# Sign rows by memset, channel angles ahead of the fold, and shared channel copies in a Fourier mixing and low-rank mixer kernel

## The chip, the cores and the metric

The kernel runs on one core of a Trainium2 chip. The metric is the device time of one execution in microseconds (us). Before the change it was 492.16 us, the median of three runs (491.61 to 494.13).

## The reference

```python
def _attn_ref(x):                       # x: 8 x 3136 x 256, float32
    X = np.fft.fft(x, axis=1)
    X = np.fft.fft(X, axis=2)
    return X.real

def _moe_ref(x, U, V, w_ch1, w_ch2):    # x: the output of the above
    xt = x.transpose(0, 2, 1)
    h = xt @ U @ V                      # U: 3136 x 32, V: 32 x 3136
    u = x + h.transpose(0, 2, 1)
    ch = np.maximum(u @ w_ch1, 0.0) @ w_ch2   # 256 -> 1024 -> 256
    return u + ch
```

For each of eight batches, the real part of a two-dimensional Fourier transform is taken; then a rank-32 mixing along the sequence is added, and then a two-layer network over the channels.

## The kernel before

**The Fourier part as products.** The sequence transform is a matrix product with cosine and sine tables that the kernel makes itself at its start: `tabs` (two tiles, sine `tabs` and cosine `tabc`, of 99 partitions by 8 by 2 by 425). Columns up to `NQ` = 393 hold the trigonometric values, the last 32 hold the tables' product with U, so one product gives the transform and U's part of the low-rank path together. VectorE computes the angles (`phase`: a multiply-add, then a mask on the integer bits, two instructions), ScalarE takes the sines (`sine`) and, with Abs before it, the cosines (`cosine`). Symmetries save sines: `mirror_even` fills half of a row from the other half, and `cosine_odd`, `cosine_low`, `cosine_high` copy sine values reversed into the cosine table. `turned_copy` gives a copy with sign + to GpSimd and one with sign - to ScalarE. `halve` scales one row of a table on VectorE. `fold_u` and `transform_u` contract U with the tables on TensorE.

**Folding x.** The rows of x come in twice, forward (`xf`, by an indirect gather issued by GpSimd) and reversed (`xr`); a 99th partition holds the edge row (`load_0f`, `load_0r`). VectorE folds along the channels (`along_d`, L303 and L305, into `EOF_` and `EOR_`), GpSimd converts two columns that stand alone (`alone`, L309), VectorE folds along the sequence (`mirror`, L312, into `EOS`), and `half` (L316) gives `G`, the stationary operand of the sequence product.

**One batch.** `transform(b)` yields eight `seq` groups (L352; each pair of groups is evicted by ScalarE into `ev` at L356 and combined by VectorE at L359, L366 and L368 or L370 into `tab`, `A` and `B`), then eight `chan` steps (L467 and L469, with the channel tables `MC` and `MSN`; each result is copied out of PSUM at L471 into `S` or `T`), then `lowrank` (L479, with `MSN` and `MC`; the result goes into `TA` at L485); in batch 0 `lowrank` stands ahead of the `chan` steps. PSUM tiles of the tag `dft` rotate through three buffers. Row 0 of `MSN` is replaced by alternating signs (L687, L688) after its sines. `TA[s]` is the stationary operand of the low-rank product with `VA[s]` (V and two more rows); its rows 32 and 33 are written by `ta_rows`: a clear, a copy of two rows of alternating signs from `alt` (L641), then a row of zeros and two single elements.

**The stream.** `front(c)` forms a chunk of 512 rows: the low-rank product `ph` (L511) plus `S` or `T` on VectorE (L519) gives `u`, which a DMA also transposes. `first_product` (L531, relu on ScalarE at L533) and `second_product` (L547, added up on VectorE at L553 to L556) are the network. Steps of the next batches (its fold, its transform, the loads of the batch after it) are spread between the products of the chunks by `spread`.

**Order.** Up to the first chunk the order of each engine's queue is the program's own (`manual_schedule`); from the second chunk on a scheduler may move instructions, with the folds and loads pinned. Every engine works through its queue in order. The loads of batch 1 and of the weights and V are issued by GpSimd, between its copies and memsets:

```python
    load_r(1, 0)
    load_f(1, 0)
    along_d(1, xr, EOR_, 1)
    load_r(1, 1)
    av = alt.rearrange("p (l two) -> p l two", two=2)
    nc.gpsimd.memset(av[:, :, 0:1], 1.0)
    nc.gpsimd.memset(av[:, :, 1:2], -1.0)
    ta_rows(0)
```

In the built program the copy at L641 carries waits for the landing of a gather of x (for `ta0` that of `load_f(1, 0)`, for `ta1` that of `load_f(1, 1)`), beside the wait for GpSimd's own clear.

Of the kernel before, what the change touches and what calls it, by code (L numbers as in the profile page):

```python
# [20 lines left out]
NQ = 393  # L21
# [6 lines left out]
def kernel(  # L28
# [227 lines left out]
    def halve(t):  # L256
        nc.vector.tensor_single_scalar(tabs[t][:, NI - 1, :, :NQ], tabs[t][:, NI - 1, :, :NQ],
                                       hv[:KP], op=AL.mult)

    def cells(t, i, col, step, n, skew):  # L260

        v = tabs[t][:, i, :, :]
        return bass.AP(v.tensor, v.offset + col, [v.ap[0], [QW + skew, 2], [step, n]])

    def turned_copy(dst, src, sgn):

        if sgn > 0:
            nc.gpsimd.tensor_copy(dst, src)  # L268
        else:
            nc.scalar.activation(dst, src, AF.Copy, scale=-1.0)  # L270
# [6 lines left out]

    def cosine_odd(i):

        turned_copy(cells(1, i, 1, 1, NQ - 1, 0), cells(0, i, NQ - 2, -1, NQ - 1, 1),  # L280
                    1 if i % 4 == 0 else -1)

    def cosine_low(i):

# [22 lines left out]
    def alone(a, src, dst):  # L307

        pin(nc.gpsimd.tensor_copy(dst[:, a, :, 128:257:128], src[:, a, :, 0:129:128]))  # L309
# [67 lines left out]
    GC = [cpool.tile([KP, NI, NB], BF16, name=f"gc{par}", tag=f"gc{par}") for par in range(2)]  # L377
    rows = cpool.tile([NB, S], BF16, name="rows")
    tabc128 = cpool.tile([NB, NB, R], BF16, name="tabc128")
    alt = cpool.tile([P, 256], BF16, name="alt")  # L380
    flip = cpool.tile([P, 2, P], BF16, name="flip")
    unit = cpool.tile([P, NB], FP32, name="unit")

# [78 lines left out]
    def chan(b, ch, h):  # L462
        d = ST[b]
        lo = ch * 392 + (1 if ch else 0)
        hi = (ch + 1) * 392 + 1
        pt = psum.tile([P, NQ], FP32, tag="dft", name="pst", bufs=3)
        nc.tensor.matmul(pt[:, :hi - lo], MC[:, h * P:(h + 1) * P], d["A"][:, lo:hi],  # L467
                         start=True, stop=False)
        nc.tensor.matmul(pt[:, :hi - lo], MSN[:, h * P:(h + 1) * P], d["B"][:, lo:hi],  # L469
                         start=False, stop=True)  # L470
        nc.scalar.copy(d["ST"[h]][:, lo:hi], pt[:, :hi - lo])  # L471

    def lowrank(b):
        d = ST[b]
# [129 lines left out]
            mirror_even(0, 3)  # L604
    cosine_low(1)
    mirror_even(0, 1)
    for i in (0, 4):
        cosine_odd(i)
    halve(0)
    nc.vector.tensor_copy(GU[:, 0], pf[0][:])  # L610
    pf.append(fold_u(1))
    nc.vector.tensor_single_scalar(sel.rearrange("p a c -> p (a c)"),
# [2 lines left out]
    us[0]()  # L615
    cosine(tabs[1][:, 7, :, NH - 1:NQ], phe[:, 0], 15)
    nc.scalar.copy(cells(1, 7, 0, 1, NH - 1, 1), cells(1, 7, NQ - 1, -1, NH - 1, 0))
    nc.scalar.copy(GU[:, 1], pf[1][:])
    us[1]()
    us[2]()  # L620
# [2 lines left out]
    cosine_low(5)  # L623
    cosine_high(1)
    us[3]()
    alone(0, xr, EOR_)
    alone(0, xf, EOF_)
    nc.gpsimd.iota(pint[:], pattern=[[0, 1]], base=D, channel_multiplier=-1)  # L628
# [3 lines left out]
    w1t = gen.tile([P, H], FP32, name="w1t", tag="w1t", bufs=1)  # L632
    gather(w1t[:], moe_w_ch1, D, pint[:], H, 0)
    alone(1, xf, EOF_)
    nc.gpsimd.memset(VA[0][:].bitcast(I32), 0)
    nc.gpsimd.dma_start(out=VA[0][:R, :], in_=moe_V)
    nc.gpsimd.dma_start(out=W2[:], in_=moe_w_ch2.rearrange("(j p) d -> p j d", p=P))

    def ta_rows(s):
        nc.gpsimd.memset(TA[s][:].bitcast(I32), 0)  # L640
        nc.gpsimd.tensor_copy(TA[s][R:R + 2, :], alt[R:R + 2, :])  # L641
        nc.gpsimd.memset(TA[s][R:R + 1, :], 0.0)
        nc.gpsimd.memset(TA[s][R:R + 1, 0:1], 1.0)
        nc.gpsimd.memset(TA[s][R:R + 1, P:P + 1], -1.0)

    for part in range(2):
        along_d(0, xr, EOR_, part)
    along_d(0, xf, EOF_, 0)
    mirror(0, slice(0, 128), AL.subtract)
    along_d(0, xf, EOF_, 1)  # L650
    mirror(0, slice(128, 258), AL.add)
    halve(1)
    for step in uc:
        step()
    along_d(1, xr, EOR_, 0)
    along_d(1, xf, EOF_, 0)
    mirror(1, slice(0, 128), AL.subtract)
# [6 lines left out]
    load_f(1, 0)  # L664
    along_d(1, xr, EOR_, 1)
    load_r(1, 1)
    av = alt.rearrange("p (l two) -> p l two", two=2)
    nc.gpsimd.memset(av[:, :, 0:1], 1.0)
    nc.gpsimd.memset(av[:, :, 1:2], -1.0)
    ta_rows(0)  # L670
    along_d(1, xf, EOF_, 1)
    mirror(1, slice(128, 256), AL.add)
    for par in range(2):
        half(0, par, slice(128, 256))
    nc.vector.memset(lrow[:, 1, 0:1], 128.0)
    nc.vector.tensor_single_scalar(pcol[:], pcol[:], 1.0 / D, op=AL.mult)
    pd = gen.tile([P, 2 * P], I32, name="pd", bufs=1)
    phase(pd[:], lrow.rearrange("p a l -> p (a l)"), pcol[:], 17)
    sine(MSN[:, 0:128], pd[:, 0:128], 17, -1)
    sine(MSN[:, 128:256], pd[:, 128:256], 17, 1)  # L680
    cosine(MC[:], pd[:], 17)
    msr = MSN[0:1].rearrange("p (l two) -> p l two", two=2)
    MDT = [MSN, MC]
    load_f(1, 1)
    load_0f(x, xf, 1, D, nc.gpsimd)
    load_0r(x, xr, 1, D, nc.gpsimd)
    nc.gpsimd.memset(msr[:, :, 0:1], 1.0)  # L687
    nc.gpsimd.memset(msr[:, :, 1:2], -1.0)  # L688
    nc.gpsimd.tensor_copy(W1[:, 1, :], w1t[:])
    ta_rows(1)  # L690
    column_zeros()
    for par in range(2):
        nc.gpsimd.memset(G[1][par][:, :, 258:GW].bitcast(I32), 0)
# [80 lines left out]
```

## Time and profile before

| | |
|---|---|
| median of three runs | 492.16 us (491.61 to 494.13) |
| profiled execution | 492.97 us |
| its span, first to last instruction | 491.2 us |
| mean granted TensorE clock | 0.979 |
| TensorE (PE) busy | 462.7 us, 94% |
| VectorE (DVE) busy | 314.4 us, 64% |
| ScalarE (ACT) busy | 282.3 us, 57% |
| GpSimd (POOL) busy | 70.2 us, 14% |

The lines that follow come from one profiled execution. In a timeline a row is: start in us from the span's start, length in us, engine, source line, operation, output<-inputs, shape, count, and in brackets the idle time before it with what ended it. In the list of waits a row is: who waited <- for whom: us in total, times, the longest. In the windows a row is: the stretch, its length, the busy time of PE, PEld (weight loads), DVE, ACT and POOL with their instruction counts, the mean granted TensorE clock, the mean busy share of the 16 DMA engines and GB/s. A matmul row's end is modelled, so lengths of rows overlap where matmuls follow each other; starts are safer.

### The profile page before, as it was taken

To read this page: it belongs to the slowest core of one execution; us is meant where nothing else is said; L and a number is where in the kernel's file an instruction comes from. 1 tells how busy PE (TensorE), PEld (TensorE's weight loads), DVE (VectorE), ACT (ScalarE), POOL (GpSimd) and SP (SyncE) were. 2 spreads that over 40 slices of the span, in tenths; PEclk is the share of its full clock that TensorE was granted. 3 is DMA by queue.
4 is the path that set the end of the run, shared out by engine and by line. 5 is a ranking of instruction groups with operands and counts; after the bars stand their busy time and mean duration, and the time that the engine had idled before them with its cause. 6 is when DMAs were issued, how large, how long until landed. Compare 5 with 4: busy or idle time off the path is not lost.

```text
span 491.2 us, 7944 instructions
## 1 busy us (share of the span) xinstructions
PE 462.7 (94%) x2979; PEld 295.3 (60%) x3033; DVE 314.4 (64%) x709; ACT 282.3 (57%) x534; POOL 70.2 (14%) x122
## 2 busy tenths in 40 slices
PE   4683999999999999999999999999999999999997
PEld 2431465665566666666666666666666666666665
DVE  8971797676677756786477657776569643344343
ACT  7621753665566655665566555655566556665562
POOL 4943431020001200121011200130000000000000
PEclk9877899999999999999999999999999999999999
DMA  7596398997347953767356833785233423343433
GB/s 197 119 193 176 62 213 150 216 179 164 66 117 190 218 87 107 196 184 143 84 146 184 220 85 87 197 224 104 84 89 78 118 64 87 107 87 108 129 87 128
DMA packets 103606, 67.24 MB, mean 137 GB/s; under 512 B 73546, under 2 KB 100068, under 8 KB 100416
## 3 DMA queue, kind: packets, MB, share of 16 engines
q1 hardware_dynamic: 97722, 40.69, 36.8%
q0 software_dynamic: 5824, 26.03, 19.9%
q8 instruction: 23, 0.38, 0.3%
q14 instruction: 15, 0.12, 0.1%
q10 hardware_dynamic: 22, 0.02, 0.0%
HBM read 29.33 MB, written 25.69 MB: 112 GB/s over the span
## 4 chain that ended last, share of the span: by engine, by line
PE 86%; DVE 5%; POOL 3%; DMA 3%; issue 2%; ACT 1%; DVEq 0%; POOLq 0%
PE p L547 34%; PE p L531 31%; PE pt L352 9%; PE ph L511 4%; DMA xf<-in_x_dram,xidx 3%; PE pst L467 3%; PE pst L469 2%; PE ptt L479 1%; PE ptc L438 1%; DVE u L519 1%; ACT tabs L177 1%; DVE pho L172 1%; POOL tabc L268 1%; DVE pho L170 0%; DVE eof L305 0%
## 5 line engine op out<-in xcount | busy, mean ns | idle before, releaser
L533 ACT ACTIVATE h<-p 128x512 bf16<-128x512 f32 x392 | 224.6, 599 | 153.7 <-PE p L531 145.1
L531 PE MATMUL p<-u,w 128*128 128x512 bf16 x732 | 208.5, 379 | 1.2 <-DVE u L519 0.3
L547 PE MATMUL p<-w,h 128*128 128x256 bf16 x1568 | 203.1, 273 | 1.5
L547 PEld LDWEIGHTS <-h 128*128 128x128 bf16 x1568 | 153.1, 98 | 59.4 <-DVE o L556 0.3
L531 PEld LDWEIGHTS <-w 128*128 128x128 bf16 x784 | 75.5, 98 | 53.6 <-issue 2.7
L553 DVE TENSOR_TENSOR o<-p,ut 128x4 f32<-128x4 f32 (+1 forms) x100 | 16.4, 164 | 93.1 <-PE p L547 87.6
L352 PEld LDWEIGHTS <-g 98*128 98x128 bf16 (+1 forms) x288 | 28.7, 100 | 30.8 <-issue 4.7
L359 DVE TENSOR_TENSOR tab<-pt,ev 128x32 bf16<-128x32 f32 x32 | 6.1, 191 | 59.1 <-PE pt L352 57.0
L55 POOL DMA_INDIRECT xf<-in_x_dram,xidx x16 | 17.8, 1110 | 170.6 <-DVE eof L305 160.5
L519 DVE TENSOR_TENSOR u<-ph,S 128x512 bf16<-128x512 f32 (+15 forms) x64 | 34.9, 554 | 11.2 <-ACT T L471 11.2
L555 DVE TENSOR_TENSOR o<-p,ut 128x254 f32<-128x254 f32 (+1 forms) x100 | 40.5, 405 | 0.0
L556 DVE TENSOR_TENSOR o<-p,ut 128x254 f32<-128x254 f32 (+1 forms) x100 | 40.4, 404 | 0.0
L352 PE MATMUL pt<-tabc,g 98*128 98x425 bf16 (+1 forms) x160 | 36.2, 355 | 0.2
L519 DVE TENSOR_TENSOR u<-ph,T 128x512 bf16<-128x512 f32 (+15 forms) x64 | 34.8, 554 | 0.0
L352 PE MATMUL pt<-tabs,g 98*128 98x425 bf16 (+1 forms) x128 | 30.0, 358 | 2.5 <-DVE g L316 1.7
L511 PE MATMUL ph<-va,ta 128*128 128x512 bf16 (+13 forms) x126 | 29.3, 332 | 0.1
L356 ACT COPY ev<-pt 128x425 f32<-128x425 f32 x32 | 16.4, 515 | 16.6 <-PE pt L352 15.4
L467 PE MATMUL pst<-A,mc 128*128 128x392 bf16 (+1 forms) x64 | 22.3, 348 | 0.3
L312 DVE TENSOR_TENSOR eos<-eof,eor 99x1024 bf16<-99x1024 bf16 (+2 forms) x33 | 22.3, 688 | 0.3 <-POOL pint L628 0.2
L469 PE MATMUL pst<-B,msn 128*128 128x392 bf16 (+1 forms) x64 | 22.2, 347 | 0.0
L316 DVE TENSOR_TENSOR g<-eos 99x2064 bf16<-99x2064 bf16 (+2 forms) x20 | 19.9, 1011 | 0.1
L303 DVE TENSOR_TENSOR eof<-xf 99x1016 bf16<-99x1016 f32 x16 | 19.9, 1244 | 0.0
(136 smaller groups left out, 300.8 us busy)
## 6 DMA issues: line engine op xcount, KB each, us to landing
out_dram<-o SPq DMA_DIRECT2D x48, 512.0 KB
xr<-in_x_dram POOLq DMA_DIRECT2D x14, 784.0 KB, 6.6
xr<-in_x_dram SPq DMA_DIRECT2D x2, 784.0 KB
ut<-u SPq DMA_TRANSPOSE x49
w<-in_moe_w_ch_dram POOLq DMA_DIRECT2D x1, 512.0 KB, 8.0
out_dram<-o SPq DMA_DIRECT2D x4, 128.0 KB
va<-in_moe_V_dram POOLq DMA_DIRECT2D x2, 196.0 KB, 3.7
xf<-in_x_dram,xidx POOLq DMA_INDIRECT x16, 7.2
```

The costliest lines, as they stand in the source:

```text
L303: pin(nc.vector.tensor_tensor(dst[:, a, :, 1:128], lo, hi, op=AL.subtract))
L312: pin(nc.vector.tensor_tensor(EOS[:, a, :, cols], EOF_[:, a, :, cols], EOR_[:, a, ::-1][:, :, cols], op=op))
L352: nc.tensor.matmul(pt[:], g[:kp(i), i, col:col + P], tabs[t][:kp(i), i, par, :], start=(n == 0), stop=(n == len(mm) - 1))
L467: nc.tensor.matmul(pt[:, :hi - lo], MC[:, h * P:(h + 1) * P], d["A"][:, lo:hi], start=True, stop=False)
L469: nc.tensor.matmul(pt[:, :hi - lo], MSN[:, h * P:(h + 1) * P], d["B"][:, lo:hi], start=False, stop=True)
L511: nc.tensor.matmul(ph[:, col:col + hi - lo], TA[b % 2][:, s * P:(s + 1) * P], VA[b % 2][:, lo:hi], start=True, stop=True)
L519: nc.vector.tensor_tensor(u[:, s, col:col + hi - lo], ph[:, col:col + hi - lo], src, op=AL.add)
L531: nc.tensor.matmul(p1[:], W1[:, s, j * P:(j + 1) * P], k["u"][:, s, :], start=(s == 0), stop=(s == 1))
L533: LAST[0] = nc.scalar.activation(k["h"][:, j, :], p1[:], AF.Relu)
L547: nc.tensor.matmul(p2[:, t % w, :], h[:, j, rs], W2[:, j, :], start=(j == 0), stop=(j == JT - 1))
L555: nc.vector.tensor_tensor(o[:, ts, 1:P], p2[:, :w, 1:P], ut[:, ts, 1:P], op=AL.add)
L556: nc.vector.tensor_tensor(o[:, ts, P + 1:D], p2[:, :w, P + 1:D], ut[:, tT, P - 1:0:-1], op=AL.add)
```

## The change

- `alt`, both `TA` tiles' constant rows and `VA[0]`'s clear are written right after the other constants, in GpSimd's queue ahead of its first table copies; the two rows of alternating signs in `TA` are now two memsets (`signs_along`), not a copy from `alt`.
- `MSN`'s sign row is written right ahead of V's load.
- The cast of W1's lower half stands right behind the third load of batch 1.
- The channel angles (`pd`, four VectorE instructions) are computed right after `halve(0)`, `MSN`'s sines after the evictions of U's first contraction and `MC` after U's second.
- `cosine_odd` is always ScalarE's, also for sign + (rows 0 and 4); `cosine_odd(0)` stands behind the cosines of row 7, `cosine_odd(4)` behind the eviction `us[3]`.
- `halve(1)` stands two VectorE instructions earlier.
- In batch 0 the four `T` copies of `chan` go to VectorE; the four `S` copies stay with ScalarE.

```diff
@@ -161,9 +161,25 @@
     VA = [cpool.tile([P, S], BF16, name=f"va{s}", tag=f"va{s}") for s in range(2)]
     TA = [cpool.tile([P, 256], BF16, name=f"ta{s}", tag=f"ta{s}") for s in range(2)]
     pint = cpool.tile([P, 1], I32, name="pint")
+    alt = cpool.tile([P, 256], BF16, name="alt")
     MSN = cpool.tile([P, 256], BF16, name="msn")
     MC = cpool.tile([P, 256], BF16, name="mc")
     nc.vector.tensor_scalar(ncol[:], ncol[:], 1.0 / S, 0.0, op0=AL.mult, op1=AL.max)
+
+    def signs_along(t):
+
+        v = t.rearrange("p (l two) -> p l two", two=2)
+        nc.gpsimd.memset(v[:, :, 0:1], 1.0)
+        nc.gpsimd.memset(v[:, :, 1:2], -1.0)
+
+    signs_along(alt)
+    for s in range(2):
+        nc.gpsimd.memset(TA[s][:].bitcast(I32), 0)
+        signs_along(TA[s][R:R + 2])
+        nc.gpsimd.memset(TA[s][R:R + 1, :], 0.0)
+        nc.gpsimd.memset(TA[s][R:R + 1, 0:1], 1.0)
+        nc.gpsimd.memset(TA[s][R:R + 1, P:P + 1], -1.0)
+    nc.gpsimd.memset(VA[0][:].bitcast(I32), 0)
 
     def phase(y, a_ap, col_ap, bits):
 
@@ -277,8 +293,8 @@
 
     def cosine_odd(i):
 
-        turned_copy(cells(1, i, 1, 1, NQ - 1, 0), cells(0, i, NQ - 2, -1, NQ - 1, 1),
-                    1 if i % 4 == 0 else -1)
+        nc.scalar.activation(cells(1, i, 1, 1, NQ - 1, 0), cells(0, i, NQ - 2, -1, NQ - 1, 1),
+                             AF.Copy, scale=1.0 if i % 4 == 0 else -1.0)
 
     def cosine_low(i):
 
@@ -377,7 +393,6 @@
     GC = [cpool.tile([KP, NI, NB], BF16, name=f"gc{par}", tag=f"gc{par}") for par in range(2)]
     rows = cpool.tile([NB, S], BF16, name="rows")
     tabc128 = cpool.tile([NB, NB, R], BF16, name="tabc128")
-    alt = cpool.tile([P, 256], BF16, name="alt")
     flip = cpool.tile([P, 2, P], BF16, name="flip")
     unit = cpool.tile([P, NB], FP32, name="unit")
 
@@ -468,7 +483,8 @@
                          start=True, stop=False)
         nc.tensor.matmul(pt[:, :hi - lo], MSN[:, h * P:(h + 1) * P], d["B"][:, lo:hi],
                          start=False, stop=True)
-        nc.scalar.copy(d["ST"[h]][:, lo:hi], pt[:, :hi - lo])
+        (nc.vector.tensor_copy if b == 0 and h == 1 else nc.scalar.copy)(
+            d["ST"[h]][:, lo:hi], pt[:, :hi - lo])
 
     def lowrank(b):
         d = ST[b]
@@ -604,9 +620,11 @@
             mirror_even(0, 3)
     cosine_low(1)
     mirror_even(0, 1)
-    for i in (0, 4):
-        cosine_odd(i)
     halve(0)
+    nc.vector.memset(lrow[:, 1, 0:1], 128.0)
+    nc.vector.tensor_single_scalar(pcol[:], pcol[:], 1.0 / D, op=AL.mult)
+    pd = gen.tile([P, 2 * P], I32, name="pd", bufs=1)
+    phase(pd[:], lrow.rearrange("p a l -> p (a l)"), pcol[:], 17)
     nc.vector.tensor_copy(GU[:, 0], pf[0][:])
     pf.append(fold_u(1))
     nc.vector.tensor_single_scalar(sel.rearrange("p a c -> p (a c)"),
@@ -615,6 +633,7 @@
     us[0]()
     cosine(tabs[1][:, 7, :, NH - 1:NQ], phe[:, 0], 15)
     nc.scalar.copy(cells(1, 7, 0, 1, NH - 1, 1), cells(1, 7, NQ - 1, -1, NH - 1, 0))
+    cosine_odd(0)
     nc.scalar.copy(GU[:, 1], pf[1][:])
     us[1]()
     us[2]()
@@ -623,6 +642,9 @@
     cosine_low(5)
     cosine_high(1)
     us[3]()
+    cosine_odd(4)
+    sine(MSN[:, 0:128], pd[:, 0:128], 17, -1)
+    sine(MSN[:, 128:256], pd[:, 128:256], 17, 1)
     alone(0, xr, EOR_)
     alone(0, xf, EOF_)
     nc.gpsimd.iota(pint[:], pattern=[[0, 1]], base=D, channel_multiplier=-1)
@@ -632,26 +654,21 @@
     w1t = gen.tile([P, H], FP32, name="w1t", tag="w1t", bufs=1)
     gather(w1t[:], moe_w_ch1, D, pint[:], H, 0)
     alone(1, xf, EOF_)
-    nc.gpsimd.memset(VA[0][:].bitcast(I32), 0)
+    signs_along(MSN[0:1])
     nc.gpsimd.dma_start(out=VA[0][:R, :], in_=moe_V)
     nc.gpsimd.dma_start(out=W2[:], in_=moe_w_ch2.rearrange("(j p) d -> p j d", p=P))
-
-    def ta_rows(s):
-        nc.gpsimd.memset(TA[s][:].bitcast(I32), 0)
-        nc.gpsimd.tensor_copy(TA[s][R:R + 2, :], alt[R:R + 2, :])
-        nc.gpsimd.memset(TA[s][R:R + 1, :], 0.0)
-        nc.gpsimd.memset(TA[s][R:R + 1, 0:1], 1.0)
-        nc.gpsimd.memset(TA[s][R:R + 1, P:P + 1], -1.0)
 
     for part in range(2):
         along_d(0, xr, EOR_, part)
     along_d(0, xf, EOF_, 0)
     mirror(0, slice(0, 128), AL.subtract)
+    halve(1)
     along_d(0, xf, EOF_, 1)
     mirror(0, slice(128, 258), AL.add)
-    halve(1)
     for step in uc:
         step()
+    cosine(MC[:], pd[:], 17)
+    MDT = [MSN, MC]
     along_d(1, xr, EOR_, 0)
     along_d(1, xf, EOF_, 0)
     mirror(1, slice(0, 128), AL.subtract)
@@ -664,30 +681,14 @@
     load_f(1, 0)
     along_d(1, xr, EOR_, 1)
     load_r(1, 1)
-    av = alt.rearrange("p (l two) -> p l two", two=2)
-    nc.gpsimd.memset(av[:, :, 0:1], 1.0)
-    nc.gpsimd.memset(av[:, :, 1:2], -1.0)
-    ta_rows(0)
+    nc.gpsimd.tensor_copy(W1[:, 1, :], w1t[:])
     along_d(1, xf, EOF_, 1)
     mirror(1, slice(128, 256), AL.add)
     for par in range(2):
         half(0, par, slice(128, 256))
-    nc.vector.memset(lrow[:, 1, 0:1], 128.0)
-    nc.vector.tensor_single_scalar(pcol[:], pcol[:], 1.0 / D, op=AL.mult)
-    pd = gen.tile([P, 2 * P], I32, name="pd", bufs=1)
-    phase(pd[:], lrow.rearrange("p a l -> p (a l)"), pcol[:], 17)
-    sine(MSN[:, 0:128], pd[:, 0:128], 17, -1)
-    sine(MSN[:, 128:256], pd[:, 128:256], 17, 1)
-    cosine(MC[:], pd[:], 17)
-    msr = MSN[0:1].rearrange("p (l two) -> p l two", two=2)
-    MDT = [MSN, MC]
     load_f(1, 1)
     load_0f(x, xf, 1, D, nc.gpsimd)
     load_0r(x, xr, 1, D, nc.gpsimd)
-    nc.gpsimd.memset(msr[:, :, 0:1], 1.0)
-    nc.gpsimd.memset(msr[:, :, 1:2], -1.0)
-    nc.gpsimd.tensor_copy(W1[:, 1, :], w1t[:])
-    ta_rows(1)
     column_zeros()
     for par in range(2):
         nc.gpsimd.memset(G[1][par][:, :, 258:GW].bitcast(I32), 0)
```

## The prediction

> **What bounds the kernel now.** I read the page first, then the windows, the waits, and the timelines of the four engines in the first 76 us. The page's busy row and one long window say what the steady stage is:
>
> ```profile
> PE 462.7 (94%) x2979; PEld 295.3 (60%) x3033; DVE 314.4 (64%) x709; ACT 282.3 (57%) x534; POOL 70.2 (14%) x122
> 100.00:470.00 370.00, 367.41 (x2421) 237.87 (x2466) 233.39 (x534) 221.72 (x421) 29.75 (x48) 1.00 0.53 130
> ```
>
> The window's columns are length, busy us of PE, PEld, DVE, ACT, POOL, clock, DMA share, GB/s. From 100 to 470 us PE is busy 367.41 of 370 at full clock: nothing is to be had there, and nothing of an earlier start is lost there. The change touches the opening only. In the list of waits of the first 60 us two rows belong together:
>
> ```profile
> POOL ta L641 <- DMA xf<-in_x_dram,xidx: 14.2, 2, 11.9
> PE ptt L479 <- POOL msn L688: 8.1, 1, 8.1
> ```
>
> GpSimd's timeline shows the link (start, length, engine, line, idle time before):
>
> ```profile
> 6.89 0.21 POOL L133 IOTA pcol<- 128x1 f32 x1
> 12.00 0.51 POOL L268 COPY tabc<-tabs 99x392 bf16<-99x392 bf16 x1 [4.89 <-ACT tabs L177]
> ...
> 15.62 3.59 POOL L268 COPY tabc<-tabs 99x784 bf16<-99x784 bf16 x2
> ...
> 21.75 0.62 POOL L631 DMA_DIRECT2D w<-in_moe_w_ch_dram  x1
> ...
> 24.34 1.41 POOL L635 MEMSET va<- 128x1568 int32 x1
> 26.04 0.55 POOL L636 DMA_DIRECT2D va<-in_moe_V_dram  x1 [0.29 <-POOL va L635]
> ...
> 30.76 0.25 POOL L640 MEMSET ta<- 128x128 int32 x1
> 42.90 0.39 POOL L641 COPY ta<-alt 2x256 bf16<-2x256 bf16 x1 [11.89 <-DMA xf<-in_x_dram,xidx]
> 43.35 0.30 POOL L642 MEMSET ta<- 1x256 bf16 x1
> ...
> 44.03 1.02 POOL L55 DMA_INDIRECT xf<-in_x_dram,xidx  x1 [0.19 <-issue]
> ...
> 46.42 0.23 POOL L688 MEMSET msn<- 1x128 bf16 x1
> ```
>
> The copy of alt into ta at 42.90 stands 11.89 us behind batch 1's first gather, which its data does not need. Queued behind it are the second gather (44.03), the sign row of msn (46.42) and W1's lower half. PE waits for that sign row:
>
> ```profile
> 25.84 1.60 PE L352 MATMUL pt<-tabs,g 98*128 98x425 bf16 x4 [1.65 <-DVE g L316]
> ...
> 46.70 0.59 PE L479 MATMUL ptt<-msn,tab 128*32 128x256 bf16 x2 [8.14 <-POOL msn L688]
> ...
> 52.86 0.33 PE L467 MATMUL pst<-A,mc 128*128 128x392 bf16 x1
> ...
> 53.19 1.92 PE L531 MATMUL p<-u,w 128*128 128x512 bf16 x7
> ...
> 72.88 0.81 PE L531 MATMUL p<-u,w 128*128 128x512 bf16 x3 [0.27 <-DVE u L519]
> ```
>
> The idle stretch also lost the clock:
>
> ```profile
> 28.40:31.84 3.44, 3.44 (x11) 1.41 (x10) 3.30 (x8) 0.00 (x0) 2.57 (x5) 0.50 0.91 118
> ...
> 38.66:42.08 3.42, 0.00 (x0) 0.00 (x0) 1.16 (x3) 0.00 (x0) 0.00 (x0) 1.00 0.84 194
> 48.90:52.32 3.42, 3.42 (x11) 1.44 (x10) 1.26 (x2) 1.92 (x5) 1.99 (x9) 0.50 0.05 12
> 52.32:55.70 3.38, 3.33 (x16) 1.55 (x16) 1.75 (x5) 3.29 (x8) 2.55 (x5) 1.00 0.67 106
> ```
>
> PE is idle from 38.66 to 42.08; after that the channel products run at 0.50 until 52.32. So 6.5 us (46.70 to 53.19) go for work that needs about half of it at full clock. VectorE and ScalarE in the same stretch:
>
> ```profile
> 7.89 0.57 DVE L172 TENSOR_SCALAR pho<-pho 99x786 int32<-99x786 int32 x1
> ...
> 13.04 0.69 DVE L610 CAST gu<-pf 99x512 bf16<-99x512 f32 x1 [1.16 <-PE pf L207]
> ...
> 16.66 1.84 DVE L303 TENSOR_TENSOR eof<-xf 99x1016 bf16<-99x1016 f32 x1
> ...
> 31.01 0.06 DVE L675 MEMSET lrow<- 128x1 f32 x1
> ...
> 31.56 0.29 DVE L172 TENSOR_SCALAR pd<-pd 128x256 int32<-128x256 int32 x1
> ...
> 39.24 0.58 DVE L368 TENSOR_TENSOR A<-ev,pt 128x392 bf16<-128x392 f32 x1
> ...
> 56.57 1.21 DVE L303 TENSOR_TENSOR eof<-xf 99x1016 bf16<-99x1016 f32 x1
> ```
>
> ```profile
> 9.48 0.86 ACT L270 ACTIVATE tabc<-tabs 99x784 bf16<-99x784 bf16 x1
> ...
> 20.87 0.32 ACT L252 ACTIVATE tabs<-put,hv 99x64 bf16<-99x64 f32 x1
> 22.70 0.49 ACT L239 CAST wu<-pu 128x393 bf16<-128x393 f32 x1 [1.51 <-PE pu L233]
> 24.22 0.54 ACT L251 CAST tabc<-put 98x448 bf16<-98x448 f32 x1 [1.03 <-PE put L246]
> ...
> 31.88 0.69 ACT L177 ACTIVATE msn<-pd,c 128x128 bf16<-128x128 int32 x2 [6.91 <-DVE pd L172]
> ...
> 33.42 0.91 ACT L356 COPY ev<-pt 128x425 f32<-128x425 f32 x2
> ...
> 48.52 0.49 ACT L471 CAST S<-pst 128x393 bf16<-128x393 f32 x1 [0.35 <-PE pst L469]
> ```
>
> VectorE's last row of batch 0 ends at 39.82, so PE could have gone on about 7 us before 46.70.
>
> **Sign rows by memset.** GpSimd's gap is 7.10 to 12.00. Into it go alt (two, each bounded by 0.23 and 0.30), per ta one clear of 0.25, two short rows by the 0.23 of L688, one row of 0.30 and two single elements (my estimate: 1.2 with the waits between), and va's clear of 1.41: 0.5 + 2.4 + 1.4 = 4.3 us, ending at 11.4. If the cover is short by as much, the mirror copies at 12.00 start later by that, and the two copies that leave the queue (next paragraph) repay it. VectorE's phases (7.89 is one) run beside these memsets. I price that at nothing; the other end, each memset holding VectorE up in full, is one of the rivals.
>
> What goes: the copy at 42.90 and its wait. In the changed program's order nothing on GpSimd between the third x load and the second gather waits for x; W1's cast is there and waits for its own gather only. The sign row of msn now stands ahead of V's load and waits for ScalarE's sines.
>
> **Two cosine copies on ScalarE.** GpSimd loses 3.59 us, ScalarE gains 2 x 0.86 (row 9.48, same shape). The first fits before the copy of gu, for which ScalarE waits. The second follows the row at 20.87: 21.19 to 22.05; then both sines, 0.69, to 22.75. The second U contraction ends on that second copy; the copy of its result, at 22.70 before, now comes after the sines and a contraction that began later, at about 23.0. PE's turn of it, which ended at 24.22, ends at about 24.5, and PE is free for batch 0.
>
> Beside GpSimd's copies VectorE's row at 16.66 took 1.84, the same work at 56.57 took 1.21. Between 0.6 (this row alone) and 1.9 (it and its two neighbours alike) comes back with the copies gone, or nothing if the stretch has another cause; I take 1.5, since the copies span all three. The first g, for which PE waited until 25.84, is there by about 24.3, and the fold ends at 29.5 instead of 31.0.
>
> **Angles ahead of the fold.** The four VectorE steps at 31.01 to 31.85 now lie in the 1.16 us before 13.04: free. ScalarE's sines and MC (31.88 to 33.42) no longer stand before the copies of ev.
>
> **The sequence products.** They start at 24.5 instead of 25.84. The clock came back 6.0 us into the stream (31.84); with the earlier start I bound its return by 28.4 and 31.84. In the first case the 32 products of the first half end near 32.2, in the second near 33.9; with VectorE's 1.2 us per pair (two rows like 39.24) its last A row ends at 36.4 or 38.0 instead of 39.82. [...]
>
> **Channel products.** PE pauses for about 0.3 us instead of 8.14, so the clock stays. At 0.17 us each (two between 52.86 and 53.19) the 16 products, ptt and two ph take 3.6 us. Sharing the copies: ScalarE 4 x 0.49, VectorE 4 x 0.58 at most (row 39.24; 0.40 at least) beside its u rows. On ScalarE alone 8 x 0.49 = 3.9 would pace PE, so sharing brings at most 0.5, and nothing if the clock is low. VectorE paces the end: p starts at 40.0 or 41.6 instead of 53.19, 11.6 to 13.2 earlier.
>
> **What is late next.** VectorE's fold of batch 1 started at 56.57, 3.4 after p, and paced PE up to 72.88. It needs batch 1's rows, with the edge row that is issued behind the second gather. These windows show the loads:
>
> ```profile
> 22.50:44.50 22.00, 13.12 (x60) 6.36 (x57) 13.78 (x29) 4.69 (x11) 9.04 (x16) 0.73 0.87 179
> 45.50:49.50 4.00, 2.80 (x10) 1.27 (x10) 0.00 (x0) 1.18 (x3) 2.30 (x6) 0.50 0.71 209
> ```
>
> W1 (21.75) is issued about 3.0 us earlier, V (26.04) about 2.8, because it now waits for the sines. The 22 us of loads so end near 41.5, and the second gather, issued near 30, adds its 4 us: 45.5 at the latest, 43.2 if the edge row overtakes. I take 45.2, near the late end since the share was already 0.87. The fold moves by 56.57 - 45.2 = 11.4 us, p by a little more; the smaller sets the end.
>
> **Sum.** The profiled execution took 492.97 us, 1.77 outside its span of 491.2; it is 0.8 above the median of 492.16. 491.2 - 11.4 = 479.8 of span, 481.6 with what lies around it, and 480.8 against the median. What can be told from no change is about 0.5%, 2.5 us.
>
> **Rivals.**
> - Loads are in time and PE alone sets the pace: p's full 13.2 us, 479.0. For it: the second gather leaves 14 us earlier. Against it: the DMA share of 0.87. Chance 0.17.
> - The stall moves but part stays: batch 1 lands near 49, because the last gather shares the engines with W2 and the first transposes of u, or the clock drops again. 56.57 - 49 = 7.6 us, 484.6. For it: loads that began to leave at 21.75 were still landing when the copy got through at 42.90. Chance 0.13.
> - The memsets hold up VectorE's phases. If each shuts VectorE out for its whole length, the 4.3 us come on top of the phases, less the 1.16 idle us before gu: 3.1 later, 483.9. For it: a VectorE row beside GpSimd's copies was stretched by half (16.66). Against it: those copies read, the memsets only write. Chance 0.07. [...] No row of this trace shows a memset beside a phase.
> - Slower: batch 1's rows land after 56.57. VectorE then stands in order at the fold, u and o queue behind it, PE runs out of u. The gain is gone from a landing at 56.57 on; at 60 it gives 491.2 + 3.4 + 1.8, relative to the median 495.6. Against it: the last gather would need 30 us from issue. Chance 0.05.
> - The change does not do what it says: a DMA wait stands on another GpSimd instruction ahead of msn's sign row, and PE still goes on near 46.7: within 1 us, 491.5. The order of the changed program shows no such wait. Chance 0.03.
>
> **How the numbers follow.** Forecast 0.55. Faster by over 0.5%: 0.55 + 0.17 + 0.13 + 0.07 = 0.92; within: 0.03; slower: 0.05. The range of 478.5 to 485.5 holds the forecast and the first three rivals, with 0.5 to 0.9 around their ends for the unknown cost of memset and PSUM copy rows, and leaves out the last two.
>
> **What would show it.** Right: no GpSimd wait for x between 31 and 42; ta and alt memsets done before 12.0; ptt at 35 to 37 without a wait for msn; clock 1.00 through the channel products; p's first at 40 to 41.6; batch 1's fold at 43 to 46, its first row waiting for DMA. Wrong: a clock of 0.50 after 36, the fold at 49 or later, phase rows clearly over 0.57 between 7 and 12, or PE idle between 40 and 75 by more than the 1.5 us or so of before.

## The result, and the profile after

The changed kernel takes 485.53 us (median; 484.87 to 486.24) against 492.15 us beside it: a ratio of 0.9858 [0.9827, 0.989], so 6.6 us faster. The forecast was 480.8, with a range of 478.5 to 485.5: the measured time lies at the very end of it. The profiled execution took 485.87 us, 1.77 outside a span of 484.1. (Two numbers below come with executions that were 7 to 8 us longer than others of the same kernel: the profile of the first experiment, of which only the opening's rows are read, and the median of the last experiment, of whose four executions two were so.)

The busy row of the page and the steady stage in the windows (length, busy us of PE, PEld, DVE, ACT, POOL, clock, DMA share, GB/s), changed kernel:

```profile
PE 461.5 (95%) x2979; PEld 294.9 (61%) x3033; DVE 318.4 (66%) x713; ACT 282.6 (58%) x532; POOL 69.2 (14%) x122
100.00:470.00 370.00, 367.42 (x2420) 237.79 (x2464) 229.89 (x529) 221.69 (x420) 26.65 (x44) 1.00 0.52 129
```

From 100 to 470 us PE is busy 367.42 of 370, as before (367.41). The whole difference lies in the opening. Its waits (us in total, times, longest), first 80 us of the changed kernel:

```profile
POOL eof L325 <- DMA xf<-in_x_dram: 20.3, 2, 12.6
DVE eof L319 <- DMA xf<-in_x_dram: 3.8, 1, 3.8
PE p L547 <- DVE u L535: 3.1, 2, 2.9
```

The rows of the copy of alt and of PE behind msn's sign row are gone. In their place stands one chain: VectorE waits for the edge row of batch 1 (GpSimd's casts wait for it too), and PE waits for VectorE's u. GpSimd's timeline of the changed kernel (start, length, engine, line, idle time before):

```profile
10.95 1.57 POOL L182 MEMSET va<- 128x1568 int32 x1
12.63 0.51 POOL L284 COPY tabc<-tabs 99x392 bf16<-99x392 bf16 x1
...
19.54 0.77 POOL L325 CAST eor<-xr 99x16 bf16<-99x16 f32 x1 [2.03 <-DMA xr<-in_x_dram]
20.21 0.62 POOL L653 DMA_DIRECT2D w<-in_moe_w_ch_dram  x1
...
24.48 0.98 POOL L659 DMA_DIRECT2D w<-in_moe_w_ch_dram  x1
...
30.71 1.25 POOL L55 DMA_INDIRECT xf<-in_x_dram,xidx  x1 [0.20 <-POOL w L684]
31.96 0.66 POOL L77 DMA_DIRECT2D xf<-in_x_dram  x1
...
36.01 0.55 POOL L696 DMA_DIRECT2D va<-in_moe_V_dram  x1 [0.29 <-POOL va L695]
49.13 1.30 POOL L325 CAST eof<-xf 99x16 bf16<-99x16 f32 x1 [12.57 <-DMA xf<-in_x_dram]
```

The second gather goes out at 30.71 instead of 44.03. The edge row (L77, 16 KB), issued at 31.96, is there only at about 49.1, 17.1 us later. In the kernel before the same load took 5.2 us from issue to landing:

```profile
45.04 0.66 POOL L77 DMA_DIRECT2D xf<-in_x_dram  x1
```

VectorE in the changed kernel:

```profile
6.72 0.92 DVE L210 TENSOR_SCALAR fl<-fl 128x256 f32<-128x256 f32 x1
...
11.21 1.53 DVE L188 TENSOR_SCALAR phe<-phe 99x394 int32<-99x394 int32 x1
...
15.26 0.67 DVE L628 CAST gu<-pf 99x512 bf16<-99x512 f32 x1
...
15.99 1.22 DVE L319 TENSOR_TENSOR eor<-xr 99x1016 bf16<-99x1016 f32 x1
...
29.46 1.61 DVE L328 TENSOR_TENSOR eos<-eof,eor 99x1024 bf16<-99x1024 bf16 x1
...
49.10 1.22 DVE L319 TENSOR_TENSOR eof<-xf 99x1016 bf16<-99x1016 f32 x1 [3.77 <-DMA xf<-in_x_dram]
```

The two rows of the kernel before that answer to the first two:

```profile
6.71 0.36 DVE L194 TENSOR_SCALAR fl<-fl 128x256 f32<-128x256 f32 x1
...
10.31 0.37 DVE L172 TENSOR_SCALAR phe<-phe 99x394 int32<-99x394 int32 x1
```

Rows beside the memsets are stretched, though not all of them, most of all the second one shown, beside va's clear of 1.57: 1.53 instead of 0.37. The cast of gu comes at 15.26 instead of 13.04. TensorE in the changed kernel, and the windows over the two spells in which its clock matters:

```profile
26.25 1.60 PE L368 MATMUL pt<-tabs,g 98*128 98x425 bf16 x4 [0.99 <-DVE g L332]
...
30.16 0.88 PE L368 MATMUL pt<-tabc,g 98*128 98x425 bf16 x4
...
36.85 0.39 PE L495 MATMUL ptt<-msn,tab 128*32 128x256 bf16 x2
...
37.77 0.34 PE L482 MATMUL pst<-A,mc 128*128 128x393 bf16 x1 [0.21 <-DVE A L382]
...
41.87 1.92 PE L547 MATMUL p<-u,w 128*128 128x512 bf16 x7
...
56.34 0.39 PE L547 MATMUL p<-u,w 128*128 128x512 bf16 x1 [2.92 <-DVE u L535]
```

```profile
28.40:31.84 3.44, 3.44 (x17) 1.70 (x16) 3.37 (x4) 0.52 (x1) 2.77 (x3) 0.80 1.18 223
57.20:60.60 3.40, 3.40 (x14) 1.84 (x13) 3.40 (x6) 1.20 (x2) 0.61 (x1) 0.51 1.13 215
```

From 28.40 to 31.84 the clock is 0.80 where it was 0.50. p starts at 41.87 instead of 53.19, 11.3 earlier. Then PE stands for 2.92 us until 56.34, and from 57.20 to 60.60 its clock is 0.51. VectorE's fold of batch 1 moved only from 56.57 to 49.10, by 7.5: 491.2 - 7.5 = 483.7, and the span is 484.1.

### The profile page after: what moved, and what is told of

Read it like the earlier page. It is cut to its first block, busy times and chain, and to the rows that moved or that the text cites. A ratio compares the mean times of both kernels' runs of the same rounds, so it can differ in the third digit from the quotient of the medians.

```text
span 484.1 us, 7947 instructions
## 1 busy us (share of the span) xinstructions
PE 461.5 (95%) x2979; PEld 294.9 (61%) x3033; DVE 318.4 (66%) x713; ACT 282.6 (58%) x532; POOL 69.2 (14%) x122
## 4 chain that ended last, share of the span: by engine, by line
PE 87%; DVE 7%; DMA 4%; issue 2%; POOL 0%; DVEq 0%; POOLq 0%
PE p L563 36%; PE p L547 32%; PE pt L368 9%; PE ph L527 4%; DMA xf<-in_x_dram 4%; PE pst L482 2%; PE pst L484 2%; PE ptt L495 1%; DVE eor L319 1%; PE ptc L453 1%; DVE eos L328 1%; DVE phe L188 1%; DVE pho L188 1%; DVE eof L321 0%; DVE eor L321 0%
## 5 line engine op out<-in xcount | busy, mean ns | idle before, releaser
L368 PE MATMUL pt<-tabs,g 98*128 98x425 bf16 (+1 forms) x128 | 29.5, 354 | 1.1 <-DVE g L332 1.0
L482 PE MATMUL pst<-A,mc 128*128 128x392 bf16 (+1 forms) x64 | 21.1, 330 | 0.8 <-DVE A L382 0.2
L484 PE MATMUL pst<-B,msn 128*128 128x392 bf16 (+1 forms) x64 | 21.1, 330 | 0.0
```

The source lines that it names most:

```text
L368: nc.tensor.matmul(pt[:], g[:kp(i), i, col:col + P], tabs[t][:kp(i), i, par, :], start=(n == 0), stop=(n == len(mm) - 1))
```

## The experiments

The theory for the missing 4.7 us: the landing of batch 1's edge row sets the end. What holds it was open: the 784 KB gather ahead of it in the queue, or other transfers that fill the DMA engines. The rival: the memsets beside VectorE's phases cost the difference. Each row's places come from one profiled execution. The landing is read from the first engine that waited for the edge row; in f4_order none did, so only a bound is known. In the last column, "sum" is 491.2 less the smaller of the two moves (p from 53.19, fold of batch 1 from 56.57), to set beside each profiled span.

| run | median us | ratio, 95% | p starts | edge row: issue, us to landing | fold starts | PE's longest wait for u | span (sum) |
|---|---|---|---|---|---|---|---|
| the kernel before | 492.15 | | 53.19 | 45.04, 5.2 | 56.57 | 0.27 | 491.2 |
| the change | 485.53 | 0.9858 [0.9827, 0.989] | 41.87 | 31.96, 17.1 | 49.10 | 2.92 | 484.1 (483.7) |
| e1_edge_first | 482.38 | 0.9789 [0.9756, 0.9822] | 42.44 | 30.43, 15.8 | 46.26 | 0.49 | not compared |
| e2_memsets_late | 486.42 | 0.9868 [0.9841, 0.9895] | 43.05 | 31.91, 17.0 | 48.95 | 1.58 | 483.6 (483.6) |
| e3_both | 482.6 | 0.9779 [0.9754, 0.9804] | 41.86 | 30.10, 16.3 | 46.39 | 0.49 | 481.1 (481.0) |
| e4_copy_only | 488.19 | 0.9896 [0.9874, 0.9919] | 45.76 | 34.02, 16.6 | 50.67 | 0.61 | 485.3 (485.3) |
| f1_w2_late | 482.45 | 0.9798 [0.9772, 0.9824] | 42.22 | 30.45, at most 10.1 | 45.60 | 0.27 | 481.2 (480.2) |
| f2_cos_pool | 486.08 | 0.9857 [0.9816, 0.9899] | 44.05 | 33.20, 15.8 | 49.06 | 0.69 | 485.2 (483.7) |
| f3_act_copies | 485.38 | 0.9872 [0.9838, 0.9906] | 43.16 | 31.97, 16.2 | 48.15 | 0.69 | 482.8 (482.8) |
| f4_order | 482.86 | 0.9814 [0.9784, 0.9844] | 42.51 | 30.07, under 7.8 | 45.89 | 0.27 | 480.5 (480.5) |
| f5_w2_only | 482.56 | 0.9781 [0.9747, 0.9814] | 43.16 | 31.91, 11.3 | 46.54 | 0.27 | 481.2 (481.2) |
| f6_angles_late | 485.65 | 0.9844 [0.9809, 0.9878] | 46.22 | 29.98, 9.9 | 49.60 | 0.27 | 485.5 (484.2) |
| f7_v2_late | 488.01 | 0.9891 [0.9799, 0.9984] | 42.44 | 32.61, 15.2 | 47.80 | 1.02 | 482.5 (482.4) |

**Edge rows first** (e1_edge_first), on the changed kernel:

```diff
-    load_f(1, 1)
     load_0f(x, xf, 1, D, nc.gpsimd)
     load_0r(x, xr, 1, D, nc.gpsimd)
+    load_f(1, 1)
```

> The changed kernel with batch 1's two edge-row loads issued ahead of its second gather instead of behind it. Theory A (queue order: the edge row waits in line behind the second gather's 784 KB, and the fold of batch 1 waits for the edge row alone): the fold's first VectorE row goes from 49.1 us to 45.3 to 46, where VectorE is free; PE's idle time before the product at 56.34 (2.9 us) and the low clock behind it go, and the time is 480.5 to 482 us. Theory B (the DMA engines are full until about 49 us with W2, x and the first transposes of u, whatever the order): the fold starts at 48 to 49 and the time stays at 485 to 486.

482.38 us, 3.2 less than the changed kernel. Its GpSimd and VectorE rows:

```profile
30.43 0.64 POOL L77 DMA_DIRECT2D xf<-in_x_dram  x1
...
46.26 1.22 DVE L319 TENSOR_TENSOR eof<-xf 99x1016 bf16<-99x1016 f32 x1 [0.35 <-DMA xf<-in_x_dram]
```

The fold starts 2.8 earlier and waits 0.35 instead of 3.77; PE's stall of 2.92 is gone. The landing is what the end hangs on. But of the 2.8 us, 1.5 come from the earlier issue; from issue to landing it still took 15.8. The gather was not the main obstacle. The 1.3 that its place may have cost are no more than the spread of this number over the runs with gather and W2 both in front (15.8 to 17.1).

**Memsets late** (e2_memsets_late): the clears and sign rows of va and the first ta go behind the memset of pint, alt and the second ta behind the last V load.

```diff
-    signs_along(alt)
-    for s in range(2):
+    def ta_rows(s):
         ...
-    nc.gpsimd.memset(VA[0][:].bitcast(I32), 0)
     ...
     nc.gpsimd.memset(pint[0:1], P)
+    nc.gpsimd.memset(VA[0][:].bitcast(I32), 0)
+    ta_rows(0)
     ...
     nc.gpsimd.dma_start(out=VA[1][:R, :], in_=moe_V)
+    signs_along(alt)
+    ta_rows(1)
```

> The changed kernel with the memsets taken out of GpSimd's gap at 7 to 12.5 us: va's clear and the first ta's rows stand ahead of the second edge copy of x (about 17.5 us), alt and the second ta's rows behind the second load of V (about 36.5 us). Theory C (a GpSimd memset shuts out a VectorE phase row for its length): no phase row of 0.37 is longer than 0.5, the copy of gu on VectorE starts at 13.0 to 13.3 instead of 15.26, and batch 0's fold ends at 29.5 to 30.5 instead of 32.3. If A or B holds as well, the fold of batch 1 still starts at 47.5 to 49 and the time falls by no more than 1 us, to 484.5 to 485.5. Rival (the phase rows are stretched by something else, or the slack hides them): gu still at 15, no change.

VectorE in this run:

```profile
11.05 0.37 DVE L186 TENSOR_SCALAR phe<-phe 99x394 int32<-99x394 int32 x1
...
13.44 0.69 DVE L626 CAST gu<-pf 99x512 bf16<-99x512 f32 x1 [0.20 <-PE pf L221]
14.18 1.52 DVE L317 TENSOR_TENSOR eor<-xr 99x1016 bf16<-99x1016 f32 x1
...
18.92 1.22 DVE L271 TENSOR_SCALAR tabc<-tabc,hv 99x786 bf16<-99x786 bf16 x1
```

The phase is back at 0.37 and gu at 13.44, so the memsets did stretch the phases: 1.8 of the 2.2 us that gu had lost. It bought nothing, 486.42, and batch 0's fold still ended at 32.3, not at the 29.5 to 30.5 expected: the fold of batch 0 now runs beside GpSimd's copies again (1.52 for the 1.22 of 15.99), a scaling row beside va's clear takes 1.22 (0.42 in the changed kernel), and the W1 load goes out at 21.75 instead of 20.21. The cost moved; the edge row, landing 17.0 after issue, decides as before.

**Both** (e3_both), the two edits together:

> Both edits of the two runs before: edge rows ahead of the second gather, memsets out of the gap. Theories A and C together: first product of the stream at 39.5 to 40.5 instead of 41.87, the fold of batch 1 at 43.5 to 45.5, 478.5 to 480.5 us. If B holds: 484.5 to 485.5.

482.6 us, no different from the edge rows alone; the 478.5 to 480.5 of the two theories together were missed. In this opening the stretched phases cost nothing that the place of the memsets could give back.

**The copy alone** (e4_copy_only): the kernel before, with only the copy of alt replaced by memsets where it stood.

```diff
-        nc.gpsimd.tensor_copy(TA[s][R:R + 2, :], alt[R:R + 2, :])
+        v = TA[s][R:R + 2].rearrange("p (l two) -> p l two", two=2)
+        nc.gpsimd.memset(v[:, :, 0:1], 1.0)
+        nc.gpsimd.memset(v[:, :, 1:2], -1.0)
```

> The kernel before with one edit: the copy of alt's two rows into ta is two memsets in the same place, so that nothing there waits for the gather of x; angles, cosine copies, channel copies and positions stay as before. Theory W (the wait behind the copy is the whole of the gain, since batch 1's edge row sets the end in either case): GpSimd runs through at 31 to 38 us, ptt at 39 to 40 at full clock, the fold of batch 1 at 48.5 to 50, 485 to 487 us. Rival (the other parts of the change carry 2 us or more of the 6.6): 488 to 490.

488.19 against 492.97 beside it: 4.8 us for this one edit. That is more than the 485 to 487 of theory W and within the 488 to 490 of its rival. TensorE and VectorE there:

```profile
45.76 1.92 PE L531 MATMUL p<-u,w 128*128 128x512 bf16 x7
50.67 1.22 DVE L303 TENSOR_TENSOR eof<-xf 99x1016 bf16<-99x1016 f32 x1 [1.45 <-DMA xf<-in_x_dram]
```

The rest of the change brings p 3.9 earlier still (41.87), but the fold only 1.6 (49.10). So it adds about 2 us, and most of what it does for PE runs into the same landing.

**W2 behind the gather, edge rows first** (f1_w2_late), on e1's kernel:

```diff
-    nc.gpsimd.dma_start(out=W2[:], in_=moe_w_ch2.rearrange("(j p) d -> p j d", p=P))
     ...
     load_f(1, 1)
+    nc.gpsimd.dma_start(out=W2[:], in_=moe_w_ch2.rearrange("(j p) d -> p j d", p=P))
```

> The changed kernel with batch 1's edge rows ahead of its second gather, and the load of W2 moved from behind V's load to behind that gather. It asks what still held the edge row until 46.3 us once it stood ahead of the gather. Theory full engines: W2 (128x8x256) is among the bytes that the edge row stands behind, so it lands 1 to 3 us earlier; the fold of batch 1 starts at 43.5 to 45.3, without a wait for DMA of over 0.4; time 480.5 to 482, at best 1.5 below edge rows first alone. Theory own queue: the edge row waits for the first gather and the x rows of its own queue whatever else moves; it lands at 46.0 to 46.5 again, time 482 to 483. Theory late weights: W2 is then late for the second products, PE waits for it at about 58 to 60, time 484 or more.

GpSimd and VectorE:

```profile
40.52 0.26 POOL L325 CAST eof<-xf 99x16 bf16<-99x16 f32 x1 [2.84 <-DMA xf<-in_x_dram]
...
45.60 1.21 DVE L319 TENSOR_TENSOR eof<-xf 99x1016 bf16<-99x1016 f32 x1
```

GpSimd, which needs the edge row too, goes on at 40.52: at most 10.1 us after issue, 5.7 less than with W2 in front. I had expected 1 to 3 us. (The 8.9 in the expectation of the next run is a misreading: it is the landing of batch 2's edge row, issued at 59.72.) Yet the time, 482.45, is that of e1: VectorE comes to the fold at 45.60 without a wait, 3.38 behind p, exactly as in the kernel before (56.57 - 53.19). The loads are now out of the path, and p's own start is the bound.

**W2 alone** (f5_w2_only): the same move on the changed kernel, edge rows still behind the gather.

> The changed kernel with one move alone: W2's load behind batch 1's second gather and edge rows; the edge rows stay behind the gather. With the edge rows first, taking W2 out of their way brought their landing from 15.8 to 8.9 us after issue. Theory full engines (W2's bytes stand in the way whatever the order): the edge row is issued at 31.2 to 32.0 and lands 9 to 12 us later, at 40.5 to 44; VectorE's fold starts at 45.4 to 46 without a wait for DMA, PE's wait of 2.92 for u is gone; time 482 to 483. Theory gather ahead (the 784 KB in front of it in the queue hold it, W2 only adds): it lands at 46 to 48, VectorE waits 0.5 to 2, time 483 to 485.

```profile
30.45 1.63 PE L368 MATMUL pt<-tabc,g 98*128 98x425 bf16 x4
...
43.16 1.92 PE L547 MATMUL p<-u,w 128*128 128x512 bf16 x7
```

```profile
43.21 0.25 POOL L325 CAST eof<-xf 99x16 bf16<-99x16 f32 x1 [5.78 <-DMA xf<-in_x_dram]
46.54 1.21 DVE L319 TENSOR_TENSOR eof<-xf 99x1016 bf16<-99x1016 f32 x1
```

The first fence is TensorE, the second GpSimd and VectorE. 482.56 us; the edge row lands 11.3 after issue, behind the gather, and nobody on the path waits for it. So W2's load ahead of it was the larger cause: 5.7 us with the edge rows first, 5.8 with them behind the gather, and both landings lie far outside the 15.8 to 17.1 of the runs with W2 in front. The 1.2 to 1.3 that the gather in front adds are no more than that spread. Whether W2 holds the edge row by its bytes in the engines or by its place in the same queue isn't told apart: the move changes both, and it also lets the first gather out 1.2 to 1.4 us earlier. Either remedy recovers the same 3 us, and both together no more. The TensorE rows also show the clock: at 30.45 four products still took 1.63, where the changed kernel, started at the same 26.2, took 0.88 at 30.16.

**Edge rows, gather, cast, W2** (f4_order), on f1's kernel: W1's cast, too, moved behind the gather.

```diff
-    nc.gpsimd.tensor_copy(W1[:, 1, :], w1t[:])
     ...
     load_f(1, 1)
+    nc.gpsimd.tensor_copy(W1[:, 1, :], w1t[:])
     nc.gpsimd.dma_start(out=W2[:], in_=moe_w_ch2.rearrange("(j p) d -> p j d", p=P))
```

> The changed kernel with batch 1's edge rows ahead of its second gather, W1's cast behind that gather and W2's load behind the cast. GpSimd issues the edge rows at about 29.5 instead of 30.4 to 31 and the gather 1.5 earlier. Theory full engines: the fold of batch 1 starts at 43 to 45 with no wait for DMA, and p at 41.9 sets the pace; time 480 to 481.5. Theory own queue: the edge row lands 0.9 to 1.2 earlier than with edge rows first alone, because it was issued so much earlier; fold at 45.2 to 45.4, time 481 to 482. Rival: W1's lower half comes late, PE waits for it, p starts at 43 or later, time 483 or more.

GpSimd takes the edge row without a wait:

```profile
37.86 0.27 POOL L325 CAST eof<-xf 99x16 bf16<-99x16 f32 x1
```

482.86 us. The loads are earlier again, and nothing follows from it: p starts at 42.51.

**Cosine copies back on GpSimd** (f2_cos_pool): `cosine_odd` and its place as before the change, the rest changed.

> The changed kernel with the two odd cosine copies back on GpSimd, where they stood before. Theory of the prediction: beside them VectorE's fold rows of batch 0 stretch again to 1.5 to 1.8 (1.20 to 1.22 without them), GpSimd's loads go out 1.9 later (its two copies of 1.8 less the 2.03 that it waits for xr anyway, so between 0 and 3.6), the edge row of batch 1 lands 1 to 3 later; time 486.5 to 488.5. Rival: GpSimd waits 2.03 for xr anyway and VectorE's rows hide behind PE; the edge row sets the end as before, at 49.1 plus at most 0.5; time 485 to 486.

VectorE and TensorE:

```profile
15.97 1.84 DVE L319 TENSOR_TENSOR eor<-xr 99x1016 bf16<-99x1016 f32 x1
...
27.50 1.60 PE L368 MATMUL pt<-tabs,g 98*128 98x425 bf16 x4 [3.53 <-DVE g L332]
```

The same row that takes 1.22 without the copies takes 1.84 beside them. The products start 1.25 later (27.50 against 26.25) and p 2.2 later, but the edge row, issued 1.2 later, still lands at 49.06 and sets the end. 486.08 us lies between the two forecasts and nearer the rival's (485 to 486): the rows stretch as the prediction's theory has it, the end is the rival's.

**All eight channel copies on ScalarE** (f3_act_copies):

```diff
-        (nc.vector.tensor_copy if b == 0 and h == 1 else nc.scalar.copy)(
-            d["ST"][h][:, lo:hi], pt[:, :hi - lo])
+        nc.scalar.copy(d["ST"][h][:, lo:hi], pt[:, :hi - lo])
```

> The changed kernel with all eight channel copies on ScalarE. Prediction: sharing is worth at most 0.5; p starts 0 to 0.5 later (41.9 to 42.4), the edge row sets the fold at 49.1 as before, time 485 to 486. Rival: freeing VectorE from its four copies brings its u rows forward; p starts 0.3 to 1 earlier, but the edge row still sets the end, time 485 to 486 too; the place of p in the trace tells them apart, the time doesn't.

```profile
39.11 0.34 PE L482 MATMUL pst<-A,mc 128*128 128x393 bf16 x1 [0.20 <-DVE A L382]
...
43.16 1.92 PE L546 MATMUL p<-u,w 128*128 128x512 bf16 x7
```

485.38 us, no difference. From the first pst product to p it takes 4.1 us with and without the sharing (39.11 to 43.16 and, in the changed kernel, 37.77 to 41.87). The sharing is worth nothing here. That p starts 1.3 later than in the changed kernel, more than the 0.5 expected, comes from ahead of these products: the clock is back at 32.5 instead of 29.8.

**Angles late** (f6_angles_late), on f1's kernel: the phase, sines and MC back behind the fold, msn's sign row behind the last loads.

> Edge rows first and W2 late, with the channel angles, sines and MC back behind the fold as before the change, and msn's sign row behind the last loads. Prediction: the early place is free and saves little by itself; late, VectorE's four steps (0.8) come after the fold and ScalarE's four (about 1.5) stand before its ev copies, and PE has its products to do meanwhile: p starts 0 to 0.8 later than 42.2, time 482.4 to 483.2. Rival: the early steps cost what they save, since U's first contraction and gu come earlier without them; p starts earlier by up to 0.8, time 481.6 to 482.4.

A miss, and a plain one: 485.65, 3.2 us more by the medians (2.3 by the ratios), where I had expected at most 0.8. The profile is of the longest of its four executions, 487.32. ScalarE, TensorE and a window:

```profile
32.99 0.69 ACT L193 ACTIVATE msn<-pd,c 128x128 bf16<-128x128 int32 x2 [7.42 <-DVE pd L188]
...
34.53 0.91 ACT L372 COPY ev<-pt 128x425 f32<-128x425 f32 x2
...
35.07 1.15 PE L368 MATMUL pt<-tabs,g 98*128 98x425 bf16 x4 [1.66 <-ACT ev L372]
...
35.60:39.00 3.40, 3.40 (x11) 1.50 (x10) 1.80 (x5) 0.00 (x0) 1.56 (x2) 0.50 1.10 214
```

ScalarE waits until 32.99 for the angles, which VectorE now makes behind the fold; the sines and MC then stand before the ev copies, which come at 34.53 instead of 29.3. PE runs out of free result tiles, waits 1.66, and has a clock of 0.50 for 3.4 us: p starts at 46.22 instead of 42.22. The early angles, which I had folded into "free", are worth 2.3 to 3.2 us once the loads are out of the way. How much of that is the clock differs between executions: the mean granted clock of the four runs from 0.986 to 0.993, their spans from 485.5 to 482.8.

**The second V load late** (f7_v2_late): VA[1]'s clear and load out of the opening into the column loop.

```diff
-    nc.gpsimd.memset(VA[1][:].bitcast(I32), 0)
-    nc.gpsimd.dma_start(out=VA[1][:R, :], in_=moe_V)
+    due.setdefault(10, []).append(v_second)
```

> The changed kernel with VA[1]'s clear and its V load (196 KB, issued at 36.01 in the changed kernel, between batch 1's edge rows and their landing) moved into the column loop, behind the first casts of batch 1's fold. It asks what shared the engines with the edge row until 49.1. Theory bytes: 196 KB at the 188 GB/s of that stretch are 1.0 us; the edge row lands at 48.0 to 48.4, the fold there, time 484.2 to 485.2. Theory transposes: the first transposes of u, from 41.28 on, hold it, and it lands at 48.8 to 49.3 as before, time 485 to 486. Theory spread: V's 32 rows take more of the engines than their bytes say; it lands at 43 to 46.5, ahead of most of the transposes, time 482.4 to 483.5. A late V would show as a wait for va at batch 1's ph products.

```profile
47.80 1.22 DVE L319 TENSOR_TENSOR eof<-xf 99x1016 bf16<-99x1016 f32 x1 [1.89 <-DMA xf<-in_x_dram]
```

VectorE goes on at 47.80, 15.2 after the edge row's issue instead of 17.1. Two of the four executions took 484.48 and 484.49, the others 491.54 and 491.86, and the interval of the ratio, [0.9799, 0.9984], is too wide to say more on the time. The landing is near the theory of bytes (48.0 to 48.4), 0.2 earlier. But with V in its place and W2 and the gather in front, five profiles show 15.8 to 17.1 from issue to landing; 15.2 is only 0.6 below the lowest, so an effect of V isn't shown.

## Why the prediction was right or wrong

The direction was right, and the time lies at the end of the range, which reached that far because it took in the rivals. The size was not: 11.4 us of gain were forecast, and 6.6 came. Three of the prediction's own signs of being wrong came: the fold at 49 or later (49.10), a phase row clearly over 0.57 (1.53), and PE idle beyond the former 1.5 us or so (2.92).

- **The copy's wait, and PE behind msn's sign row: right.** GpSimd runs through from 28.86 to 36.6 without a wait for x, where the copy of alt stood until 42.90; its next wait, 12.57 until 49.13, is for batch 1's edge row. ptt starts at 36.85 (35 to 37 forecast); PE pauses 0.21 us where 8.14 stood, and the channel products run at full clock (1.00 from 36.85 to 41.87).
- **Memsets priced at nothing: wrong in the row.** They end at 12.5 rather than 11.4, and VectorE comes to gu 2.2 later, of which e2 gives 1.8 back. That is the rival to which I gave 0.07, and the stretch it named is shown: the phase row at 11.21 took 1.53 beside a memset of 1.57, and 0.37 in e2, with that memset moved. Why this row is held up and another is not (at 9.46 one took 0.37 beside memsets of 0.37 and 0.38) no run shows. My argument against it, that memsets only write, was no protection. Its price is another matter: with the memsets elsewhere the time was the same.
- **The copies' return of 1.5: right.** f2 shows 1.25 at the first product. But the fold of batch 0 ended at 32.4, not 29.5: 2.2 for gu, and 0.9 for an eos row that now lies beside W1's cast (29.46: 1.61 instead of 0.69), which I had moved without asking who runs beside it.
- **The products and the clock: late.** They start at 26.25, not 24.5. A's last row ended at 38.2, p started at 41.87: 0.2 and 0.3 past the late ends. The bounds for the clock's return, 28.4 and 31.84, were my estimate, and no run shows 28.4: with the same start of the products (26.2 to 26.3) it came back at 29.8 in the changed kernel, 30.5 in f1, 31.2 in f4 and 32.5 in f3 and f5, the last two past the late bound, and p followed (41.87, 42.22, 42.51, 43.16, 43.16).
- **Angles ahead of the fold: right in direction, mis-sized.** I named ScalarE's copies of ev and gave them no term; f6 shows 2.3 to 3.2 us for it, on f1's kernel, by a wait of PE and by the clock.
- **Sharing the copies:** at most 0.5 forecast, nothing measured.
- **What is late next: the step that failed.** I let batch 1's rows land at 45.2, the fold there; they landed at 49.1. That is 3.9 of the missing 4.7. The rule of the sum held (11.4 of forecast became 7.5 by the same subtraction, and it gives eight of the table's eleven spans within 0.4, the other three within 1.0 to 1.5). The mis-sized term is the landing of the last loads. I moved the 22 us of loads as a block, with the gather's 4 us after them, although the 4 us were read behind 44.03, when the gather before had landed (it released the copy of alt at 42.90) and the edge row took 5.2 us. Issued at 30.71, the same gather and edge row stand behind W2, which alone costs the edge row 5.7 to 5.8 us (f1, f5).
- **Two smaller terms of the same step** were off as well, and no run shows that they matter. W1 went out 1.5 us earlier (21.75 to 20.21) instead of 3.0, because GpSimd waited 2.03 for x; but in f3, whose opening is the same, it went out at 18.34, and the edge row was still issued at 31.97 and landed at 48.15. And a load joined that I had left where it was, the second V load, in the kernel before

```profile
54.01 0.55 POOL L695 DMA_DIRECT2D va<-in_moe_V_dram  x1 [0.29 <-POOL va L694]
```

  and in the changed kernel at 36.01; f7 leaves its share open.
- **The rival that came** is "the stall moves but part stays", landing near 49 and 484.6 us, to which I gave 0.13. It named W2 and the first transposes of u; W2 is shown. For the transposes (SyncE issues them from 41.28 on) no run was made; in e2, f3, f2 and e4 they begin 1.0 to 1.8 us later after the edge row's issue, and it still takes 15.8 to 17.0: no sign of a large share, and no proof against one. Nor is it settled why W2 costs nearly 6 us, where its 512 KB would pass in 2.8 at the 188 GB/s of 20 to 45 us. These are the bytes written, in bf16; the load reads W2 as float32, twice as much, and whether that counts no run shows.
- **What is left of 480.8:** with the landing out of the path (f1, f4, f5) the time is 482.4 to 482.9, 1.6 to 2.1 above the forecast. p's start explains 0.4 to 1.4 of it by the sum: it moved by 11.0, 10.7 and 10.0 us instead of 11.4, with VectorE's later fold and the clock's return. The rest is no more than executions of one kernel differ by.

## What to carry to other kernels

When a blocking wait goes, the loads behind it are issued earlier, here into fuller engines (the DMA share from 20 to 45 us rose from 0.76 to 1.02): price their landing by what is in flight at the new time, not by how fast they landed at the old one (here 5.2 us before, with the gather alone just ahead, and 17.1 after), and put loads that are needed late (here W2 at its old place) behind the ones needed first. A removed wait pays only up to the next late arrival (here p moved by 11.3 us, batch 1's fold by 7.5, the span by 7.1), so write the sum as the smaller of the moves of each candidate and look which one each later edit touches. And price an idle gap of TensorE with its clock: here gaps of 1.66 and 2.92 us were each followed by 3.4 us at half speed, a further 1.7 us, and one of 1.58 us by none.

## What the runs showed that I had not expected

- After a gap of 2.92 us (the changed kernel) and one of 1.66 us (f6), TensorE ran at 0.50 to 0.51 for 3.4 us although it was busy throughout; a gap of 1.58 us in e2 left the clock at 1.00. Half speed for 3.4 us is 1.7 us of work. In the first half of batch 0's products the clock's return differs by 2.7 us between equal starts (29.8 in the changed kernel, 32.5 in f3 and f5); what sets it no run shows.
- A 16 KB load took 17.1 us from issue to landing, where it had taken 5.2; with one 512 KB load out of its way, 10.1 to 11.3.
- Two kernels with the loads early (f1, f4) and one with them barely in time (e1) take the same time within 0.5 us: once p's start is the bound, edge rows that land 6 to 8 us earlier buy nothing.
